# Attention and channel MLP on one core: exponentials written to SBUF, a new order of the work, kv rows added in pairs for the first batch, weights converted at other places

## The chip, the cores and the metric

The kernel runs on one core of a Trainium2 chip. The metric is the device time of one execution in microseconds; here it is the median of several runs. A core has five engines that run on their own and wait for each other through semaphores: TensorE (PE in the profile, its weight loads PEld), VectorE (DVE), ScalarE (ACT), GpSimd (POOL) and SyncE (SP, which here only issues DMAs). SBUF is the working memory, PSUM the small memory into which TensorE writes.

## The reference, cut to what matters

```python
kv_pool = kv.reshape(B, H//4, 4, W//4, 4, C).mean(axis=(2, 4))   # 16 rows averaged into one
k = v = kv_pool.reshape(B, -1, C) @ w_sr                          # 768 keys per batch
s = q @ k.T / sqrt(C)                                             # 12288 queries per batch, 4 batches
a = softmax(s)
x = a @ v
x_prev = x shifted down by one row (zeros first)
xk = mu_k*x + (1-mu_k)*x_prev;  xr = mu_r*x + (1-mu_r)*x_prev
out = sigmoid(xr @ w_r) * (relu(xk @ w_k)**2 @ w_v)               # w_k is 128x1024, w_v 1024x128
```

The inputs q, kv and w_sr are float32, the other weights float64. The output has to be more exact than one pass of TensorE's reduced float32 (`fp32r`) gives, so the kernel splits each operand into a high and a low part and adds three products.

## The kernel before, in words

The 4 x 12288 queries are cut into 96 **tiles** of 512, 24 to a batch. For one tile the work runs through these steps; the names in brackets are those of the table `WHEN`, and a digit counts the four groups of 128 queries (s) or the four pairs of 128 MLP columns (f).

- q is loaded (`qf`) and split (`qh` on ScalarE, `ql` on GpSimd).
- For each s: scores for 768 keys in PSUM, six matmuls (`S0` to `S3`); their maximum on VectorE (`nm`); the exponential with its sum on ScalarE (`ex`), written **in place into the PSUM tile S** (line 270); one over the sum (`dn`, `rc`, VectorE, one column); the probabilities as two float16 halves, the high one by ScalarE (`f1`, line 289), the low one by VectorE (`f2`, line 294), both into the tile `pp`, both reading S. So S keeps its PSUM slot until `f2` has ended. A DMA on SP's queue transposes `pp` into `pT` (`tt`, line 303).
- The product with v, three matmuls for each of six key blocks, into `px` (`AV0` to `AV5`).
- `xe` (ScalarE), `xc`, `d`, `xk`, `xr` (VectorE) mix with the row before; both are split (`xkh` VectorE, `xrh` ScalarE, `xkl` and `xrl` GpSimd).
- The MLP: for each f, `ph` in PSUM by `ha` (four matmuls with `xkh`) and `hb` (two with `xkl`); `rr` = relu on ScalarE (`r`); `kk` = `ph` x `rr` on VectorE (`k2`); `kh` = square, rounded, on ScalarE; `kl` = `kk` - `kh` on GpSimd, for f = 3 on VectorE. `kk` is the last reader of `ph`, for f = 3 `kl` is. `va` and `vb` multiply `kh` and `kl` with w_v into `pv`.
- The gate: `z` (three matmuls into `pz`), `az`, `rl`, `E`, `th` on ScalarE, `g` on VectorE; then `o` = `pv` x `g` and the store (`so`).

**PSUM.** `S`, `ph` and the batch's `pk` and `pt` share one ring of three slots (`ps_b`, line 58). Eight tiles pass through it for each tile of queries. `px` and `pz` share one slot.

**What sets the order.** `WHEN` gives each step of tile i the time `i * PERIOD + WHEN[step]`; `PERIOD` is 20.2. All steps go through a heap in the order of these planned times (lines 491 to 494), so each engine gets its instructions in that order, and steps of up to four tiles stand between each other. The times are only a sorting key: an instruction starts when its engine reaches it and its inputs and its buffer are ready. For planned times up to `FREE` = 72 the order isn't kept, and the framework's scheduler sorts these instructions by itself (`Ordered`, line 21).

**The batch's keys.** Batch 0 (`first_pool`, line 114) loads 16 tiles of 768 kv columns; TensorE multiplies and adds the first 512 columns of each tile in PSUM (`pk`), VectorE adds the other 256 (`acc`). The other batches (`later_pool`) are summed on VectorE, one `acc` reduction in each of twelve tiles of queries. `batch_prep` then splits the keys (`ks`, `ksh`, `ksl`), scales them (`am`, `ex`, `exi`, `exs`, `ivs`, `sv`, `ksv`), transposes them on TensorE (`pt`) and splits them into float16 (`v1`, `v2`).

**The weights.** w_k, w_v and w_r come as pairs of 32-bit words. `load_weights` (line 81) converts a chunk of 512 columns by six steps on VectorE (`e`, `ef`, `ei`, `m`, `ei` again, `m` again), two on ScalarE (`lf` and the high part) and three on GpSimd (`rest`, `dw`, the low part): four such chunks and one of 128 columns.

Of the kernel before, what the change touches and what calls it, by code (L numbers as in the profile page):

```python
# [39 lines left out]
def tile_kernel(ctx, tc, qT, kv0, kvw, w_sr, mu_k, mu_r, w_k, w_v, w_r, outT):  # L40
# [39 lines left out]

    def load_weights(w, hi, lo, half):

        n = w.shape[1]
        raw = prep.tile([P, n, 2], I32, name="raw", tag="kv", bufs=KV_BUFS)
        sp.dma_start(out=raw, in_=w)
        yield 4.0
# [27 lines left out]
    def first_pool(b):  # L114

        pk = ps_b.tile([P, 1024], F32, name="pk", tag="big")
        acc = prep.tile([P, K - 512], F32, name="acc", tag="acc")
        first = None
        for w in range(WIN):
# [5 lines left out]
            if w == 0:  # L125
                dve.tensor_copy(out=acc, in_=kv_t[:, 512:K])
            else:
                dve.tensor_tensor(out=acc, in0=acc, in1=kv_t[:, 512:K], op=ALU.add)
            yield 1.1
        pe.matmul(pk[:, 512:K], lhsT=wsr, rhs=acc, start=True, stop=True)  # L130
        return pk

    def later_pool(b):

# [10 lines left out]
        yield 2.0  # L145
        return pk

    def batch_prep(b, res):
# [6 lines left out]
        for c0, c1 in [(0, K)] if later else CHUNKS:  # L155
            act.activation(out=ks[:, c0:c1], in_=pk[:, c0:c1], func=AF.Copy, scale=scale / WIN)
            if later:
                yield 3.0
            dve.tensor_copy(out=ksh[:, c0:c1], in_=ks[:, c0:c1])
            if later:  # L160
                yield 3.0
            eng = pool if later else dve
            eng.tensor_tensor(
                out=ksl[:, c0:c1], in0=ks[:, c0:c1], in1=ksh[:, c0:c1].bitcast(F32), op=ALU.subtract
            )
# [306 lines left out]

    def weights(w, hi, lo, half):
        for c in range(0, w.shape[1], WC):
            cs = slice(c, min(c + WC, w.shape[1]))
            yield from load_weights(w[:, cs, :], hi[:, cs], lo[:, cs], half)
# [56 lines left out]
}  # L533
# [56 lines left out]
```

## Time and profile before

| | us |
|---|---|
| three runs | 2091.45, 2091.7, 2087.99 (median 2091.45) |
| the profiled execution | 2088.22 |
| its span, first to last instruction | 2086.4 |
| TensorE busy | 1990.4 (95%) |
| VectorE busy | 1833.1 (88%) |
| ScalarE busy | 1795.7 (86%) |
| GpSimd busy | 1071.6 (51%) |
| first scores / first `ph` of tile 0 | at 30.82 / at 80.31 |
| one tile in the steady stretch | 20.77 |
| mean granted TensorE clock | 0.989 |

A row of the timeline has the start, the duration, the engine, the source line, the operation, output<-inputs and shapes; in square brackets stands how long the engine sat idle before it and who ended that. All instructions carry L33, the helper through which they are issued, so groups are told apart by the names of their tiles. Matmuls overlap, so a start-to-start distance tells more about TensorE than a duration. A row by groups has the count, busy time in all and mean ns of one, then idle time before them. In a row by windows, busy time of PE, PEld, DVE, ACT and POOL follows the window's length, each with a count in brackets, then the granted clock, the busy share of the DMA engines and GB/s.

### The profile page before, as it was taken

What the parts mean: (1) busy time and instruction counts of PE and PEld (TensorE: products, weight loads), DVE (VectorE), ACT (ScalarE), POOL (GpSimd) and SP (SyncE); (2) the same over time, 40 slices, a digit from 0 to 9 for tenths busy, and PEclk for the clock granted to TensorE, in tenths of its full rate; (3) what the DMA queues carried; (4) which work ended last, traced back from release to release, by engine and by line L of the source; (5) the groups of instructions that cost most, each with busy time, mean ns of one, the idle gap of its engine ahead of it and who ended that gap; (6) DMA issues with size and microseconds to landing.
All of it is one profiled execution on the core that took longest, in us unless ns stands there. A gap on an engine that the chain in (4) does not pass through costs nothing.

```text
span 2086.4 us, 27449 instructions
## 1 busy us (share of the span) xinstructions
PE 1990.4 (95%) x8998; PEld 1435.8 (69%) x8998; DVE 1833.1 (88%) x2809; ACT 1795.7 (86%) x2612; POOL 1071.6 (51%) x600
## 2 busy tenths in 40 slices
PE   5799999999999999999999999999999999999998
PEld 2467676677777777667676777766767676767676
DVE  5799998888889999889898999988888898889896
ACT  2689898889898989889898888888989898989897
POOL 2455555445555555545555555554555555555555
PEclk8799999999999999999999999999999999999999
DMA  6456564555565566445555656554645454545452
GB/s 215 91 109 144 110 143 89 97 106 104 99 126 127 127 126 129 93 83 113 93 110 126 137 119 134 111 102 89 114 89 114 89 114 89 114 89 113 90 103 51
DMA packets 638544, 230.61 MB, mean 111 GB/s; under 512 B 606401, under 2 KB 606657, under 8 KB 638401
## 3 DMA queue, kind: packets, MB, share of 16 engines
q1 hardware_dynamic: 638400, 228.85, 53.9%
q8 instruction: 72, 1.18, 0.2%
q14 instruction: 72, 0.58, 0.1%
HBM read 52.63 MB, written 25.17 MB: 37 GB/s over the span
## 4 chain that ended last, share of the span: by engine, by line
PE 85%; DVE 8%; ACT 5%; DMA 1%; issue 1%; POOL 0%; POOLq 0%; DVEq 0%; SPq 0%; ACTq 0%
PE ph L33 27%; PE pv L33 26%; PE S L33 19%; PE px L33 9%; DVE kk L33 6%; ACT rr L33 5%; PE pz L33 3%; DMA kv_t<-kv 1%; PE pk L33 1%; DVE nm L33 0%; DVE m L33 0%; DVE ei L33 0%; DVE dn L33 0%; DMA raw<-moe_w_k 0%; DVE pp L33 0%
## 5 line engine op out<-in xcount | busy, mean ns | idle before, releaser
L33 POOL TENSOR_TENSOR kl<-kk,kh 128x1024 fp32r<-128x1024 f32 x288 | 689.4, 2394 | 352.5 <-DVE kk L33 196.3
L33 ACT ACTIVATE rr<-ph 128x1024 f32<-128x1024 f32 x384 | 392.7, 1023 | 107.8 <-PE ph L33 106.1
L33 PE MATMUL px<-pT,v 128*128 128x512 f16 x1728 | 441.4, 383 | 0.9 <-ACT v L33 0.9
L33 DVE TENSOR_REDUCE nm<-S 128x1 f32<-128x768 f32 x384 | 365.9, 954 | 84.1 <-PE S L33 83.5
L33 DVE TENSOR_TENSOR kk<-ph,rr 128x1024 f32<-128x1024 f32 x288 | 351.8, 1221 | 90.5 <-ACT rr L33 85.5
L33 POOL TENSOR_TENSOR xrl<-xr,xrh 128x512 fp32r<-128x512 f32 x96 | 122.7, 1278 | 598.9 <-ACT xrh L33 598.9
L33 ACT ACTIVATE S<-S,nm 128x768 f32<-128x768 f32 x384 | 331.7, 864 | 110.3 <-DVE nm L33 110.0
L33 ACT ACTIVATE kh<-rr 128x1024 fp32r<-128x1024 f32 x384 | 409.0, 1065 | 18.0 <-ACT rr L33 0.4
L33 DVE SCALAR_TENSOR_TENSOR pp<-S,rc,pp 128x768 f16<-128x768 f32 x384 | 380.3, 1011 | 12.8 <-ACT pp L33 1.5
L33 PE MATMUL ph<-xkh,wkl 128*128 128x512 f32 x768 | 331.6, 432 | 49.0 <-DVE dn L33 44.2
L33 ACT ACTIVATE pp<-S,rc 128x768 f16<-128x768 f32 x384 | 336.7, 903 | 5.1 <-ACT S L33 5.0
L33 PE MATMUL pv<-kh,wvl 128*128 128x512 f32 x768 | 304.7, 397 | 0.4 <-ACT kh L33 0.3
L33 PE MATMUL S<-ksh,ql 128*128 128x512 f32 (+1 forms) x768 | 280.5, 366 | 25.4 <-DVE pp L33 17.3
L33 PE MATMUL pv<-kh,wvh 128*128 128x512 f32 x768 | 304.5, 397 | 0.0
L33 PE MATMUL ph<-xkh,wkh 128*128 128x512 f32 x768 | 303.8, 396 | 0.0
L33 PEld LDWEIGHTS <-v 128*128 128x128 f16 x1728 | 139.0, 98 | 197.7 <-issue 80.8
L33 PE MATMUL S<-ksl,qh 128*128 128x512 f32 (+1 forms) x768 | 260.7, 339 | 0.0
L33 PE MATMUL S<-ksh,qh 128*128 128x512 f32 (+1 forms) x768 | 260.7, 339 | 0.0
L33 PE MATMUL ph<-xkl,wkh 128*128 128x512 f32 x768 | 260.2, 420 | 0.0
L33 PEld LDWEIGHTS ph<-xkh,wkl 128*128 128x128 f32 x768 | 144.6, 188 | 134.2 <-DVE dn L33 89.0
L33 PE MATMUL pv<-kl,wvh 128*128 128x512 f32 x768 | 212.2, 397 | 0.7 <-POOL kl L33 0.6
L33 PEld LDWEIGHTS S<-ksh,ql 128*128 128x128 f32 x768 | 145.6, 190 | 64.5 <-issue 26.7
(80 smaller groups left out, 2834.2 us busy)
## 6 DMA issues: line engine op xcount, KB each, us to landing
qf<-qT SPq DMA_DIRECT2D x96, 256.0 KB, 3.0
outT<-o SPq DMA_DIRECT2D x96, 256.0 KB, 3.7
kv_t<-kvw SPq DMA_DIRECT2D x36, 512.0 KB, 4.3
kv_t<-kv SPq DMA_DIRECT2D x16, 384.0 KB, 4.1
pT<-pp SPq DMA_TRANSPOSE x384, 4.2
raw<-moe_w_k SPq DMA_DIRECT2D x2, 512.0 KB, 4.7
raw<-moe_w_v SPq DMA_DIRECT2D x2, 512.0 KB, 7.2
raw<-moe_w_r SPq DMA_DIRECT2D x1, 128.0 KB, 2.0
```

The source lines that it names most:

```text
L33: ins = op(*args, **kwargs)
```

## The change

1. `ex` writes a new SBUF tile `pe` (four buffers); `f1` and `f2` read it. S is free after `ex`.
2. `WHEN` is a new table. A tile's steps are spread over a longer time (from `S0` to `vb3` 75.9 instead of 64.0 planned units), and all of them stand in another order.
3. `FREE` is -99: the table's order holds from the first instruction on.
4. For batch 0, kv is loaded two rows at a time, first 512 columns of all, then 256; VectorE adds the two (`two`), TensorE multiplies the sum: 8 + 8 float32 matmuls instead of 16 + 1. The keys' first 512 columns are split before the rest is loaded.
5. w_k is loaded between the kv loads and its conversion starts before S0; w_v and w_r are loaded together after the first q tiles, and their steps are spread, `W_GAP` = 1.8 planned units apart. `lf` comes first of a chunk's steps after `e`.
6. The kv ring has six buffers instead of four; q of the tiles after the first isn't loaded before S0; the preparation of the next batch starts two tiles later.

```diff
-    def load_weights(w, hi, lo, half):
+    def load_weights(raw, hi, lo, half, gap):
...
+    def split(c0, c1, pk, ks, ksh, ksl):
+        act.activation(out=ks[:, c0:c1], in_=pk[:, c0:c1], func=AF.Copy, scale=scale / WIN)
+        dve.tensor_copy(out=ksh[:, c0:c1], in_=ks[:, c0:c1])
+        dve.tensor_tensor(
+            out=ksl[:, c0:c1], in0=ks[:, c0:c1], in1=ksh[:, c0:c1].bitcast(F32), op=ALU.subtract
+        )
...
-            kv_t = prep.tile([P, K], F32, name="kv_t", tag="kv", bufs=KV_BUFS)
-            sp.dma_start(out=kv_t, in_=kv0[:, w, :])
-            pe.matmul(
-                pk[:, 0:512], lhsT=wsr, rhs=kv_t[:, 0:512], start=(w == 0), stop=(w == WIN - 1)
-            )
...
+        for c0, c1 in CHUNKS:
+            for w in range(0, WIN, 2):
+                kv_t = prep.tile([P, 2, c1 - c0], F32, name="kv_t", tag="kv", bufs=KV_BUFS)
+                sp.dma_start(out=kv_t, in_=kv0[:, w:w + 2, c0:c1])
+                two = work.tile([P, T], F32, name="two", tag="az", bufs=2)[:, 0:c1 - c0]
+                dve.tensor_tensor(out=two, in0=kv_t[:, 0, :], in1=kv_t[:, 1, :], op=ALU.add)
+                pe.matmul(pk[:, c0:c1], lhsT=wsr, rhs=two, start=(w == 0), stop=(w == WIN - 2))
+                yield 1.0
+            split(c0, c1, pk, ks, ksh, ksl)
...
-                    out=st[f"S{s}"][:, :K], in_=st[f"S{s}"][:, :K], func=AF.Exp,
+                    out=new(f"pe{s}", [P, K], F32), in_=st[f"S{s}"][:, :K], func=AF.Exp,
...
-                act.activation(out=pp[:, 0, :], in_=st[f"S{s}"][:, :K], func=AF.Copy, scale=st[f"rc{s}"])
+                act.activation(out=pp[:, 0, :], in_=st[f"pe{s}"], func=AF.Copy, scale=st[f"rc{s}"])
...
-                pp, pr, rc = (st[f"{x}{s}"] for x in ("pp", "S", "rc"))
+                pp, pr, rc = (st[f"{x}{s}"] for x in ("pp", "pe", "rc"))
...
-    for k, args in enumerate((
-        (w_k, wkh, wkl, False), (w_v, wvh, wvl, True), (w_r, wrh, wrl, False),
-    )):
-        steps(W_AT + T0 + 1.1 * WIN + W_STEP * k, weights(*args))
+    steps(T0 + WK_AT, weights(0.5, (w_k, wkh, wkl, False)))
+    steps(S0 + WV_AT, weights(W_GAP, (w_v, wvh, wvl, True), (w_r, wrh, wrl, False)))
...
-            steps((i + min(3, NT - 1)) * PERIOD, batch_prep(b + 1, bps[b + 1]))
+            steps((i + min(5, NT - 1)) * PERIOD, batch_prep(b + 1, bps[b + 1]))
...
-FREE = 72.0
+FREE = -99.0
...
-KV_BUFS = 4
+KV_BUFS = 6
...
-BR_AT = 14.35
+BR_AT = 15.59
...
-    "qf": -41.330, "qh": -17.482, "ql": -1.754, "S0": 4.395, "S1": 4.870, "nm0": 5.333,
+    "qf": 2.612, "qh": 19.614, "ql": 27.757, "S0": 44.210, "nm0": 50.572, "ex0": 50.578,
```

**Where the order moves instructions.** First ScalarE, before, in the steady stretch, from `r0` of one tile to its `kh1`; the rows in between are the softmax of a later tile (`S` is the score tile, now and then both in- and output, `rr` the relu, `ph` the MLP's PSUM tile):

```order
L33 ACTIVATE rr0_1205<-ph_1185 128x1024
L33 ACTIVATE kh0_1208<-rr0_1205 128x1024
L33 CAST xrh_1213<-xr_1089 128x512
L33 ACTIVATE S_1224,sm2_1252<-S_1224,nm2_1231 128x768
L33 ACTIVATE rr1_1254<-ph_1215 128x1024
L33 ACTIVATE S_1239,sm3_1258<-S_1239,nm3_1250 128x768
L33 ACTIVATE pp2_1270<-S_1224,rc2_1265 128x768
L33 ACTIVATE xe_1283<-px_1194,sv_387 128x512
L33 ACTIVATE kh1_1293<-rr1_1254 128x1024
```

And ScalarE now, the same steps:

```order
L33 ACTIVATE pe2_3265,sm2_3266<-S_3225,nm2_3237 128x768
L33 ACTIVATE pp1_3286<-pe1_3239,rc1_3261 128x768
L33 ACTIVATE rr0_3293<-ph_3232 128x1024
L33 ACTIVATE rr1_3295<-ph_3246 128x1024
L33 ACTIVATE kh0_3299<-rr0_3293 128x1024
L33 CAST qh_3306<-qf_3119 128x512
L33 ACTIVATE pe3_3310,sm3_3311<-S_3276,nm3_3304 128x768
L33 ACTIVATE pp2_3326<-pe2_3265,rc2_3274 128x768
L33 ACTIVATE pp3_3342<-pe3_3310,rc3_3330 128x768
L33 ACTIVATE xe_3345<-px_3242,sv_313 128x512
L33 ACTIVATE kh1_3349<-rr1_3295 128x1024
```

`r0` and `r1` stand one behind the other, `ex2` ahead of both, and the exponential's output is `pe`, no longer S.

VectorE before, in the steady stretch, from `f2` of one tile (`pp0`, `pp1`, second input S) to its `f2` of the third group:

```order
L33 SCALAR_TENSOR_TENSOR pp0_1409<-S_1347,rc0_1396,pp0_1409 128x768
L33 SCALAR_TENSOR_TENSOR pp1_1417<-S_1356,rc1_1411,pp1_1417 128x768
L33 TENSOR_TENSOR kk0_1439<-ph_1404,rr0_1424 128x1024
L33 TENSOR_REDUCE nm2_1450<-S_1443 128x1
L33 TENSOR_REDUCE acc_634<-kv_t_1237 128x64
L33 TENSOR_REDUCE nm3_1469<-S_1458 128x1
L33 TENSOR_SCALAR dn2_1479<-sm2_1471 128x1
L33 RECIPROCAL rc2_1484<-dn2_1479 128x1
L33 TENSOR_TENSOR kk1_1491<-ph_1434,rr1_1473 128x1024
```

And VectorE now, the corresponding stretch:

```order
L33 TENSOR_REDUCE acc_636<-kv_t_2367 128x64
L33 RECIPROCAL rc1_2594<-dn1_2585 128x1
L33 SCALAR_TENSOR_TENSOR pp0_2592<-pe0_2519,rc0_2554,pp0_2592 128x768
L33 TENSOR_SCALAR dn2_2605<-sm2_2599 128x1
L33 RECIPROCAL rc2_2607<-dn2_2605 128x1
L33 SCALAR_TENSOR_TENSOR pp1_2619<-pe1_2570,rc1_2594,pp1_2619 128x768
L33 TENSOR_TENSOR kk0_2630<-ph_2563,rr0_2626 128x1024
L33 TENSOR_REDUCE nm3_2637<-S_2609 128x1
L33 TENSOR_TENSOR kk1_2641<-ph_2577,rr1_2628 128x1024
```

`f2` takes two SBUF tiles; between `kk0` and `kk1` only `nm3` is left; the batch's reduction `acc` stands ahead of `rc1`.

VectorE now at the start, from the last adds of kv pairs to the first maximum of tile 0 (`raw_149` and `raw_151` are the chunks of w_k, `raw_230` the first of w_v); before, every weight step stood behind the last kv add:

```order
L33 TENSOR_TENSOR two_190<-kv_t_188 128x256
L33 SCALAR_TENSOR_TENSOR ei_184<-raw_149,ei_184 128x512
L33 TENSOR_TENSOR m_186<-m_186,ei_184 128x512
L33 TENSOR_TENSOR two_197<-kv_t_195 128x256
L33 TENSOR_SCALAR e_206<-raw_151 128x512
L33 TENSOR_SCALAR ef_210<-e_206 128x512
L33 CAST ksh_98<-ks_97 128x256
L33 TENSOR_TENSOR ksl_99<-ks_97,ksh_98 128x256
L33 TENSOR_SCALAR ei_228<-ef_210 128x512
L33 TENSOR_SCALAR m_238<-raw_151 128x512
L33 SCALAR_TENSOR_TENSOR ei_228<-raw_151,ei_228 128x512
L33 TENSOR_TENSOR m_238<-m_238,ei_228 128x512
```

One chunk of w_k is done, and another begun, before the keys are split; the other steps stand among tile 0's and tile 1's softmax.

More of the change, by code (lines that the diff above doesn't have):

```diff
@@ L79, in tile_kernel @@
     WC = 512
-    def load_weights(w, hi, lo, half):
[L83 to L86, printed above, removed]
+    def load_weights(raw, hi, lo, half, gap):
+        n = raw.shape[1]
         l32, h32 = raw[:, :, 0], raw[:, :, 1]
@@ L89, in load_weights @@
         dve.tensor_scalar(e, h32, 20, 0x7FF, op0=ALU.logical_shift_right, op1=ALU.bitwise_and)
+        lf = work.tile([P, n], F32, name="lf", tag="kl", bufs=3)
+        act.activation(out=lf, in_=l32.bitcast(mybir.dt.uint32), func=AF.Copy, scale=2.0 ** -52)
+        yield gap
         least = 897.0 if half else 896.0
@@ L92, in load_weights @@
         dve.tensor_scalar(ef, e, least, least + 255.0, op0=ALU.max, op1=ALU.min)
+        yield gap
         ei = work.tile([P, n], I32, name="ei", tag="kk", bufs=2)
         dve.tensor_scalar(ei, ef, least, 2.0 ** 23, op0=ALU.subtract, op1=ALU.mult)
+        yield gap
         m = work.tile([P, n], I32, name="m", tag="rr", bufs=2)
         dve.tensor_scalar(m, h32, 0xFFFFF, 3, op0=ALU.bitwise_and, op1=ALU.logical_shift_left)
-        lf = work.tile([P, n], F32, name="lf", tag="kl", bufs=3)
-        act.activation(out=lf, in_=l32.bitcast(mybir.dt.uint32), func=AF.Copy, scale=2.0 ** -52)
-        yield 2.0
+        yield gap
         dve.scalar_tensor_tensor(
@@ L102, in load_weights @@
         )
+        yield gap
         dve.tensor_tensor(out=m, in0=m, in1=ei, op=ALU.bitwise_or)
+        yield gap
         top = m.bitcast(F32)
@@ L112, in tile_kernel, with first_keys, later_keys @@
     CHUNKS = [(c, min(K, c + 512)) for c in range(0, K, 512)]
-    def first_pool(b):
-        pk = ps_b.tile([P, 1024], F32, name="pk", tag="big")
-        acc = prep.tile([P, K - 512], F32, name="acc", tag="acc")
-        first = None
-        for w in range(WIN):
-            kv_t = prep.tile([P, K], F32, name="kv_t", tag="kv", bufs=KV_BUFS)
-            sp.dma_start(out=kv_t, in_=kv0[:, w, :])
-            pe.matmul(
-                pk[:, 0:512], lhsT=wsr, rhs=kv_t[:, 0:512], start=(w == 0), stop=(w == WIN - 1)
-            )
[L125 to L133, printed above, removed]
+    def split(c0, c1, pk, ks, ksh, ksl):
[4 more added lines that the diff above has]
+        )
+    def first_keys(ks, ksh, ksl):
+        pk = ps_b.tile([P, 1024], F32, name="pk", tag="big")
+        for c0, c1 in CHUNKS:
[7 more added lines that the diff above has]
+            split(c0, c1, pk, ks, ksh, ksl)
+    def later_keys(b, ks, ksh, ksl):
         acc = prep.tile([P, K], F32, name="acc", tag="acc")
@@ L145, in later_pool @@
         yield 2.0
-        return pk
+        act.activation(out=ks, in_=pk[:, 0:K], func=AF.Copy, scale=scale / WIN)
+        yield 3.0
+        dve.tensor_copy(out=ksh, in_=ks)
+        yield 3.0
+        pool.tensor_tensor(out=ksl, in0=ks, in1=ksh.bitcast(F32), op=ALU.subtract)
     def batch_prep(b, res):
         later = b > 0
-        pk = yield from (later_pool if later else first_pool)(b)
         ks = prep.tile([P, K], F32, name="ks")
@@ L154, in batch_prep @@
         ksl = bat.tile([P, K], F32R, name="ksl")
[L155 to L165, printed above, removed]
+        yield from later_keys(b, ks, ksh, ksl) if later else first_keys(ks, ksh, ksl)
         res += [ksh, ksl]
-        yield V_WAIT
+        yield V_WAIT if later else 4.0
         am = prep.tile([P, 1], F32, name="am")
@@ L186, in batch_prep @@
         dve.tensor_scalar_mul(ksv, ks, ivs)
-        yield until(PK_AT, 4.0) if later else 1.0
+        yield until(PK_AT, 4.0) if later else 2.0
         v1 = bat.tile([P, NK, P], F16, name="v1")
@@ L221, in plan_tile, with at @@
         st = {}
-        def at(when):
+        def at(when, least=-math.inf):
             def take(fn):
-                note(i * PERIOD + when, fn)
+                note(max(i * PERIOD + when, least), fn)
             return take
@@ L231, in new @@
             return st[key]
-        @at(WHEN["qf"])
+        @at(WHEN["qf"], WHEN["S0"] if i else -math.inf)
         def _():
             sp.dma_start(out=new("qf", [P, T], F32), in_=qT[b, :, t * T:(t + 1) * T])
-        @at(WHEN["qh"])
+        @at(WHEN["qh"], WHEN["S0"] + 0.1 if i else -math.inf)
         def _():
@@ L471, in tile_kernel, with weights @@
     bps = {b: [] for b in range(B)}
[L473 to L476, printed above, removed]
+    def weights(gap, *what):
+        parts = []
+        for w, hi, lo, half in what:
+            for c in range(0, w.shape[1], WC):
+                cs = slice(c, min(c + WC, w.shape[1]))
+                raw = prep.tile([P, cs.stop - c, 2], I32, name="raw", tag="kv", bufs=KV_BUFS)
+                sp.dma_start(out=raw, in_=w[:, cs, :])
+                parts.append((raw, hi[:, cs], lo[:, cs], half, gap))
+        yield W_WAIT
+        for part in parts:
+            yield from load_weights(*part)
     S0 = WHEN["S0"]
-    T0 = S0 - 1.1 * WIN - 4.0
+    T0 = S0 - 2 * (WIN // 2) - 0.1
     steps(T0, batch_prep(0, bps[0]))
-    for k, args in enumerate((
-        (w_k, wkh, wkl, False), (w_v, wvh, wvl, True), (w_r, wrh, wrl, False),
-    )):
-        steps(W_AT + T0 + 1.1 * WIN + W_STEP * k, weights(*args))
+    steps(T0 + WK_AT, weights(0.5, (w_k, wkh, wkl, False)))
+    steps(S0 + WV_AT, weights(W_GAP, (w_v, wvh, wvl, True), (w_r, wrh, wrl, False)))
     for mu, src in ((mk, mu_k), (mr, mu_r)):
@@ L494, in tile_kernel @@
         fn()
-FREE = 72.0
-W_AT = 1.0
-W_WAIT = 5.0
-W_GAP = 1.4
+FREE = -99.0
+WK_AT = 8.1
+WV_AT = 0.1
+W_WAIT = 4.0
+W_GAP = 1.8
 V_WAIT = 16.0
```

5 lines of the change are left out of this document (2 added, 3 removed), and 30 rows, old and new, of the table WHEN.

## The prediction

> **What bounds the kernel now.** I read the page first (busy time per engine), then busy time by stretches, then the groups with what ended the idle time before them, then the timeline around the largest wait.
>
> ```profile
> PE 1990.4 (95%) x8998; PEld 1435.8 (69%) x8998; DVE 1833.1 (88%) x2809; ACT 1795.7 (86%) x2612; POOL 1071.6 (51%) x600
> ```
>
> The page's first part: TensorE is the fullest engine, but VectorE and ScalarE are not far behind. By stretches of the span:
>
> ```profile
> 0.00:30.82 30.82, 18.51 (x34) 6.23 (x35) 8.71 (x22) 3.94 (x6) 3.18 (x8) 1.00 0.83 270
> 30.82:80.31 49.49, 22.67 (x84) 16.70 (x85) 43.83 (x77) 22.90 (x40) 22.73 (x19) 0.68 0.52 111
> ```
>
> Two single periods of the steady stretch, the first with a reduction for the next batch, the second without:
>
> ```profile
> 182.27:203.04 20.77, 20.29 (x95) 14.77 (x94) 19.31 (x30) 18.54 (x27) 10.90 (x6) 1.00 0.61 127
> 980.84:1001.61 20.77, 20.29 (x95) 14.76 (x94) 18.28 (x29) 18.55 (x28) 10.90 (x7) 1.00 0.50 101
> ```
>
> After its window, a row has its length, then busy time of PE, PEld, DVE, ACT and POOL. Two things carry the time. In the steady stretch one tile (of 96) takes 20.77 us, and TensorE is busy for 20.29 of it: it is the bound, but not quite full. And until the first MLP matmul at 80.31 VectorE is the bound: 43.83 of 49.49 us.
>
> The next rows show the missing half microsecond, first as a group with its releasers, then one instance of it in the timeline.
>
> ```profile
> L33 PE MATMUL ph<-xkh,wkl 128*128 128x512 f32 x768 | 331.6, 432 | 49.0 <-DVE dn L33 44.2 <-DVE xkh L33 3.2 <-DVE kk L33 1.5
> 1016.83 0.62 PE L33 MATMUL ph<-xkl,wkh 128*128 128x512 f32 x2
> 1017.30 2.12 PE L33 MATMUL px<-pT,v 128*128 128x512 f16 x9
> 1019.90 0.50 PE L33 MATMUL ph<-xkh,wkl 128*128 128x512 f32 x1 [0.48 <-DVE dn L33]
> 1020.23 0.39 PE L33 MATMUL ph<-xkh,wkh 128*128 128x512 f32 x1
> 1020.46 0.40 PE L33 MATMUL ph<-xkh,wkl 128*128 128x512 f32 x1
> 1017.49 1.02 ACT L33 ACTIVATE rr<-ph 128x1024 f32<-128x1024 f32 x1 [0.19 <-PE ph L33]
> 1018.62 1.23 DVE L33 TENSOR_TENSOR kk<-ph,rr 128x1024 f32<-128x1024 f32 x1 [0.37 <-ACT rr L33]
> ```
>
> The wait is put down to `dn`, a tiny instruction, but what ends at 1019.85 is `kk`, the last reader of a `ph` tile (1018.62 + 1.23). So it is a wait for a PSUM slot: `hb1` fills the tile, `rr` reads it, `kk` reads it, and only then may `ha2` start: 1019.90 - 1017.30 = 2.60 us, over which the order has only nine `px` matmuls. The loss per tile is 0.48 us, and a restart of 0.10 (1019.90 to 1020.23 is 0.33, the next step 0.23).
>
> **The change part by part.** *Exponentials in SBUF, and the new order.* S now gives up its PSUM slot after `ex` instead of after `f1` and `f2`. In the new TensorE order `hb0` and `hb1` stand together, and AV2, S3, AV3, vb2, vb3 and AV4 follow before `ha2`, AV5 too before `ha3`. Lengths from neighbouring starts:
>
> ```profile
> 1011.36 0.82 PE L33 MATMUL px<-pT,v 128*128 128x512 f16 x3
> 1011.83 0.82 PE L33 MATMUL ph<-xkl,wkh 128*128 128x512 f32 x2
> 1012.49 0.82 PE L33 MATMUL px<-pT,v 128*128 128x512 f16 x3
> 1005.06 0.40 PE L33 MATMUL S<-ksh,ql 128*128 128x512 f32 x1
> 1006.11 0.39 PE L33 MATMUL S<-ksh,ql 128*128 128x512 f32 x1
> ```
>
> Three AV and two other matmuls take 1012.49 - 1011.36 = 1.13 us, 0.23 each; one S takes 1006.11 - 1005.06 = 1.05. So AV2, S3, AV3, vb2 with vb3, AV4 are 0.69 + 1.05 + 0.69 + 0.92 + 0.69 = 4.0 us. `ha2` needs `rr0` and `kk0`, the 2.60 us above: covered by 1.4. `ha3` needs `rr0`, `rr1`, then `kk0`, `nm3`, `kk1` on VectorE; from `hb1`'s end: S3 is done at 1.74, `nm3` (0.95) by about 2.9, `kk1` by 4.1, and `ha3` comes at 4.0 + `ha2` 0.92 + AV5 0.69 = 5.6. The other slots go the same way: S needs `nm` and `ex` only, 1.9 us together with no row behind it. That stall goes; what is late next is VectorE, whose rows are these:
>
> ```profile
> L33 DVE SCALAR_TENSOR_TENSOR pp<-S,rc,pp 128x768 f16<-128x768 f32 x384 | 380.3, 1011 | 12.8 <-ACT pp L33 1.5
> L33 ACT ACTIVATE S<-S,nm 128x768 f32<-128x768 f32 x384 | 331.7, 864 | 110.3 <-DVE nm L33 110.0
> L33 DVE TENSOR_REDUCE nm<-S 128x1 f32<-128x768 f32 x384 | 365.9, 954 | 84.1 <-PE S L33 83.5
> L33 DVE TENSOR_TENSOR ksl<-ks,ksh 128x512 fp32r<-128x512 f32 x1 | 0.7, 681 | 0.0
> L33 DVE TENSOR_TENSOR ksl<-ks,ksh 128x256 fp32r<-128x256 f32 x1 | 0.4, 415 | 0.0
> L33 ACT ACTIVATE kh<-rr 128x1024 fp32r<-128x1024 f32 x384 | 409.0, 1065 | 18.0 <-ACT rr L33 0.4
> L33 ACT ACTIVATE rr<-ph 128x1024 f32<-128x1024 f32 x384 | 392.7, 1023 | 107.8 <-PE ph L33 106.1
> L33 ACT ACTIVATE pz<-pz 128x512 f32<-128x512 f32 x192 | 112.1, 584 | 0.1
> L33 ACT ACTIVATE az<-pz 128x512 f32<-128x512 f32 x96 | 55.6, 580 | 0.0
> ```
>
> `f2` with both inputs in SBUF: `ksl` gives 681 + 266 = 947 ns for 768 columns, against 1011: -0.06 us, four times -0.25 per tile. `f1` from SBUF: `kh` against `rr`, +42 ns for the other source, +0.17 per tile. `ex` into SBUF: 580 ns into SBUF against 584 into PSUM, nothing. ScalarE then has 18.55 + 0.17 = 18.7 us per tile, VectorE 18.28 - 0.25 = 18.0, and 19.31 - 0.25 = 19.1 in the tiles with a reduction of the next batch (36 of 96), against TensorE's 20.2 (20.77 - 0.48 - 0.10 = 20.19; 20.29 if the restart was no loss). The Trainium skill speaks against this destination: its page "ScalarE: Activation LUTs", section "ACT is a hardware spline evaluator", says that ScalarE writes PSUM faster than SBUF. The rows 580 and 584 do not show it; by the rule `ex` would grow by an amount that the page doesn't give, and the 1.5 us that ScalarE has free per tile would take it.
>
> So the steady term is 0.48 to 0.58 us per tile. I take 0.52, since a fuller TensorE will find some small waits, over the 95 periods from the first tile's `ha0` to the last one's: -49 us, bounds -46 and -55.
>
> *The start.* `two` adds pairs on VectorE and halves TensorE's passes over kv, w_k's two transfers go between the kv loads, and its first chunk is converted before S0.
>
> ```profile
> L33 DVE TENSOR_TENSOR m<-m,ei 128x512 int32<-128x512 int32 x4 | 4.9, 1218 | 0.0
> L33 DVE TENSOR_SCALAR ei<-ef 128x512 int32<-128x512 f32 x4 | 3.3, 820 | 0.0
> L33 DVE SCALAR_TENSOR_TENSOR ei<-raw,ei 128x512 int32<-128x512 int32 x4 | 2.9, 728 | 0.0
> L33 DVE TENSOR_SCALAR m<-raw 128x512 int32<-128x512 int32 x4 | 2.9, 720 | 0.0
> L33 DVE TENSOR_SCALAR e<-raw 128x512 int32<-128x512 int32 x4 | 2.6, 654 | 1.9 <-DMA raw<-moe_w_k 1.9
> L33 DVE TENSOR_SCALAR ef<-e 128x512 f32<-128x512 int32 x4 | 2.6, 650 | 0.0
> 24.90 4.66 DMA raw<-moe_w_k
> ```
>
> ```profile
> 24.90 1.72 SPq L33 DMA_DIRECT2D raw<-moe_w_k  x2
> ```
>
> All four large chunks now lie behind the kv loads: 19.2 us of the 43.83. One whole chunk (1.22 + 0.82 + 0.73 + 0.72 + 0.65 + 0.65 = 4.8 us) and the first two steps of the next (1.3) move ahead of S0, where VectorE is busy 8.71 of 30.82 us: -6.1. The rest only changes place; it still stands ahead of tile 0's first `ha0`. The eight adds for 512 columns (0.68) and eight for 256 (0.42) come to 8.8 us, against 16 of 256 columns today (6.7): hidden under the loads. The raw transfers, 1 MB ahead of seven kv loads, cost at the 270 GB/s of the first row 3.9 us if nothing else gives; six buffers and half as many matmuls of TensorE give some back. I take S0 as unmoved, with bounds -3 and +4, and no gain from the `f2` of the first two tiles, which meet GpSimd's weight steps (below, up to +4). On SP's queue w_v's and w_r's three transfers now stand together ahead of the first `pT`: 3 x 0.86 = 2.6 us of issue (1.72 for two, above), hidden, since `f20` of tile 0 ends 0.95 + 0.86 + 0.95 = 2.8 us or more after S0 (`nm`, `ex`, itself), and the issue starts before S0. On GpSimd `ql` of tile 1 stands behind w_k's six steps; S0 of tile 1 waits longer for `ksv` and `pt` anyway. The start: -6 us, bounds -9 and +2.
>
> *The batch preparation* (two tiles later, S itself two tiles later against the plan's zero) issues the same instructions; its reduction now stands between `dn1` and `rc1`, where VectorE would otherwise wait for `rr0`. Its place in the PSUM ring can cost or save a stall like today's 2.00 us per batch:
>
> ```profile
> 395.71 0.47 PE L33 MATMUL S<-ksh,ql 128*128 128x512 f32 x1 [2.00 <-DVE v L33]
> ```
>
> Three batches: 0, bounds -6 and +6. *The end*: `vb2` and `vb3` of a tile come 12 us later after S0 in the table, but the last tile's `ha0` to the end is bound by the same chain, three `kl` on GpSimd, `o`, and the store; 0, bounds -3 and +5.
>
> Sum: -49 - 6 = -55. The profiled execution took 2088.22 us (span 2086.4), inside the three runs (2087.99 to 2091.7, median 2091.45), so 2033.
>
> **The rivals.** *Slower: VectorE waits for GpSimd.* The rows show a VectorE instruction whose operands all lie in SBUF waiting for a GpSimd instruction that has begun.
>
> ```profile
> 36.51 1.37 POOL L33 TENSOR_TENSOR rest<-lf,ei 128x512 f32<-128x512 f32 x1 [28.61 <-DVE dn L33]
> 36.68 1.75 DVE L33 TENSOR_TENSOR m<-m,ei 128x512 int32<-128x512 int32 x1
> 50.54 0.68 DVE L33 TENSOR_TENSOR m<-m,ei 128x512 int32<-128x512 int32 x1
> L33 POOL TENSOR_TENSOR kl<-kk,kh 128x1024 fp32r<-128x1024 f32 x288 | 689.4, 2394 | 352.5 <-DVE kk L33 196.3 <-ACT kh L33 149.2 <-PE pt L33 5.3
> ```
>
> The same add takes 0.68 us, or 1.75 when GpSimd began 0.17 earlier and ended at 37.88. Until now `f2` had one input in PSUM; now both are in SBUF, four per tile, 1.0 us each, beside three `kl` of 2.39 us and three smaller steps: GpSimd is busy 10.90 of 20.77. If they met by chance, an `f2` would meet a `kl` in 7.2/20.2 of cases and wait half of it (1.2), or a small step (3.7/20.2) and wait 0.6: 0.55 each, 2.2 us per tile. VectorE would have 18.0 + 2.2, and with half of its present gaps (20.77 - 18.28 = 2.5) 21.4 us per tile: 0.68 slower than now, +65 - 6, or 2147 us. It decides from about 1.5 us of waits per tile. Against it: the order. `xkl` and `xrl` wait for `xkh` and `xrh`, well ahead of `f20` and `f21`, and the first `kl` waits for `kh0` behind them, so GpSimd has nothing to run there; `f22` comes about when `kl0` ends, `f23` before `kh1` lets `kl1` go. Chance 0.10. The Trainium skill, page "SBUF — State Buffer", section "SBUF: two separate sides", states this as a rule: VectorE with two SBUF inputs and GpSimd take one port pair for a whole instruction, and the other is blocked. The rows agree for integer operands; for float32 with float16, as in `f2`, no run here shows it.
>
> *Half the gain.* The ring of three slots stalls elsewhere, say 0.26 us per tile (`hb3`, `rr3`, `kh3`, `kl3` free a slot only about 2 us before its next use): +25, 2058. Speaks for it: the old table was planned for the same period of 20.2 and came out at 20.77. Chance 0.13.
>
> *No gain in the steady stretch*, the start alone, or neither: VectorE's 19.1 us and its waits fill the period in the tiles with reductions and the ring elsewhere. 2082 to 2090. Chance 0.07, half of it within the bound.
>
> **How the numbers follow.** The forecast has 0.70: 2033, its own range from the bounds of its terms (-73 and -33), 2015 to 2055. About 0.2% (4 us) is what a measurement of this kernel can tell from no change. Faster by more: 0.70 + 0.13 + 0.04 = 0.87; same 0.03; slower 0.10. The range takes in the forecast and most of the half gain: 2015 to 2066.
>
> **What would show it.** Right: one tile takes 20.2 to 20.3 us, the wait of `ph` for VectorE is gone from the groups, first `ha0` near 74 us instead of 80.31, `f2` near 0.95 us. Wrong: `f2` with a mean well over 1.0 us (the port), a new wait of TensorE of some tenths that recurs every tile (the ring), or a first `ha0` at 80 or later.

## The result and the profile after

The changed kernel takes 2014.68 us (median of 4 runs, 2012.33 to 2015.09), the kernel before 2089.72 (the three runs of the table ahead and one more, 2087.38 to 2091.7): a ratio of 0.9639, 95% interval 0.9622 to 0.9656. The forecast was 2033 with a range of 2015 to 2066, so the time lies just below it: the sign and the mechanism came, the gain is 75 us and not 55. The profiled execution took 2014.93 us, its span 2013.2 against 2086.4.

The page's first part, engine by engine:

```profile
PE 1966.7 (98%) x8996; PEld 1430.8 (71%) x8996; DVE 1800.9 (89%) x2809; ACT 1810.1 (90%) x2612; POOL 1080.7 (54%) x600
```

Busy time by stretches: up to the first S, from there to the first MLP matmul, and one steady period.

```profile
0.00:28.81 28.81, 17.80 (x32) 7.52 (x33) 14.17 (x25) 4.24 (x6) 4.36 (x9) 0.88 0.87 297
28.81:73.83 45.02, 24.32 (x92) 17.21 (x91) 40.98 (x73) 22.20 (x40) 20.74 (x18) 0.70 0.47 100
980.64:1000.69 20.05, 20.05 (x95) 14.69 (x93) 17.89 (x29) 18.69 (x28) 10.98 (x7) 1.00 0.57 110
```

S0 starts at 28.81 (30.82 before) and the first MLP matmul at 73.83 (80.31). A period takes 20.05 us, and TensorE is busy for all of it; before it was 20.77.

The groups that the prediction priced, with the idle time ahead of each:

```profile
L33 DVE SCALAR_TENSOR_TENSOR pp<-pe,rc,pp 128x768 f16<-128x768 f32 x384 | 381.9, 1015 | 26.7 <-ACT pp L33 26.1 <-issue 0.3
L33 PE MATMUL ph<-xkh,wkl 128*128 128x512 f32 x768 | 357.0, 465 | 5.1 <-ACT pe L33 4.1 <-DVE xkh L33 0.9
L33 ACT ACTIVATE pp<-pe,rc 128x768 f16<-128x768 f32 x384 | 347.3, 933 | 11.8 <-ACT pe L33 11.2 <-DVE rc L33 0.4
L33 ACT ACTIVATE pe<-S,nm 128x768 f32<-128x768 f32 x384 | 346.8, 903 | 18.8 <-DVE nm L33 11.1
```

`ph` waits 5.1 us in all (49.0 before), so the stall of each tile is gone. `f2` takes 1015 ns (1011 before), `f1` 933 (903), `ex` 903 (864).

The last tile's `ha0` in the timeline of before; and in after's timeline the first batch's wait and, as the last row, the same `ha0`:

```profile
2068.55 0.40 PE L33 MATMUL ph<-xkh,wkl 128*128 128x512 f32 x1
```

```profile
368.78 0.82 PE L33 MATMUL pt<-ident,ksv 128*128 128x128 f32 x6
...
370.13 0.40 PE L33 MATMUL pv<-kh,wvh 128*128 128x512 f32 x1
372.96 0.50 PE L33 MATMUL S<-ksh,ql 128*128 128x512 f32 x1 [2.43 <-DVE v L33]
...
375.56 0.63 PE L33 MATMUL pv<-kh,wvl 128*128 128x512 f32 x1
375.99 0.63 PE L33 MATMUL pv<-kh,wvh 128*128 128x512 f32 x1
...
1995.34 0.47 PE L33 MATMUL ph<-xkh,wkl 128*128 128x512 f32 x1 [0.49 <-DVE xkh L33]
```

From the first `ha0` to the last one: 1988.24 us before, 1921.51 after, 66.7 less. The start gives 6.5, and from the last `ha0` to the end it is 17.85 and 17.86. That is the whole 73.2 of the span. Inside the 66.7, 95 periods x 0.714 (20.767 and 20.053, the medians over all tiles) make 67.8; the three batches cost 3.8 more than before; and the first tile's distance to the second gained 2.6 us more than a period's gain (24.10 before, 20.80 after).

The upper rows of after show a wait of the kind that the prediction left open: S waits 2.43 us for `v`, the last reader of the slot of `pt`, once for each batch, and then matmuls start every 0.43 us and not every 0.23. Over its regular periods, measured from one tile's `z` to the next one's, a batch costs 7.3 us, each of the three (6.5, 6.6 and 4.9 before).

### The profile page after: what moved, and what is told of

It reads as the page before. It is cut to its first block, busy times and chain, and to the rows that moved or that the text cites. A ratio compares the mean times of both kernels' runs of the same rounds, so it can differ in the third digit from the quotient of the medians.

```text
span 2013.2 us, 27575 instructions
## 1 busy us (share of the span) xinstructions
PE 1966.7 (98%) x8996; PEld 1430.8 (71%) x8996; DVE 1800.9 (89%) x2809; ACT 1810.1 (90%) x2612; POOL 1080.7 (54%) x600
## 4 chain that ended last, share of the span: by engine, by line
PE 93%; ACT 2%; DVE 1%; issue 0%; DVEq 0%; ACTq 0%
PE ph L33 26%; PE pv L33 26%; PE S L33 20%; PE px L33 19%; PE pz L33 3%; ACT kh L33 1%; ACT rr L33 0%; DVE kk L33 0%; ACT xe L33 0%; DVE pp L33 0%; DVE v L33 0%; DVE ph L33 0%; DVE kl L33 0%; ACT ks L33 0%; ACT v L33 0%
## 5 line engine op out<-in xcount | busy, mean ns | idle before, releaser
L33 PE MATMUL px<-pT,v 128*128 128x512 f16 x1728 | 474.4, 384 | 4.4 <-DMA pT<-pp 4.4
L33 ACT ACTIVATE rr<-ph 128x1024 f32<-128x1024 f32 x384 | 382.5, 1022 | 102.3 <-PE ph L33 101.8
L33 DVE TENSOR_TENSOR kk<-ph,rr 128x1024 f32<-128x1024 f32 x288 | 350.5, 1218 | 76.8 <-ACT rr L33 75.1
L33 DVE SCALAR_TENSOR_TENSOR pp<-pe,rc,pp 128x768 f16<-128x768 f32 x384 | 381.9, 1015 | 26.7 <-ACT pp L33 26.1
L33 ACT ACTIVATE pe<-S,nm 128x768 f32<-128x768 f32 x384 | 346.8, 903 | 18.8 <-DVE nm L33 11.1
L33 PE MATMUL ph<-xkh,wkl 128*128 128x512 f32 x768 | 357.0, 465 | 5.1 <-ACT pe L33 4.1
L33 ACT ACTIVATE pp<-pe,rc 128x768 f16<-128x768 f32 x384 | 347.3, 933 | 11.8 <-ACT pe L33 11.2
L33 PEld LDWEIGHTS <-v 128*128 128x128 f16 x1728 | 123.7, 98 | 207.3 <-issue 135.7
L33 PE MATMUL ph<-xkl,wkh 128*128 128x512 f32 x768 | 244.4, 419 | 0.0
L33 PE MATMUL pv<-kl,wvh 128*128 128x512 f32 x768 | 243.3, 419 | 0.0
L33 PEld LDWEIGHTS pv<-kl,wvh 128*128 128x128 f32 x768 | 145.2, 189 | 41.1 <-POOL kl L33 0.5
```

Source lines behind the costliest of these rows:

```text
L33: ins = op(*args, **kwargs)
```

## The experiments

**Each half of the steady change alone.** e1 is the kernel before with the exponentials in SBUF; e3 is the changed kernel with the exponentials back over S.

```diff
-                    out=st[f"S{s}"][:, :K], in_=st[f"S{s}"][:, :K], func=AF.Exp,
+                    out=new(f"pe{s}", [P, K], F32), in_=st[f"S{s}"][:, :K], func=AF.Exp,
```

(f1 and f2 read `pe`; four buffers. e3 is the reverse in the changed kernel.)

> The kernel before with one part of the change: the exponentials written to SBUF, its own order and start kept. Slot theory (the steady gain is a wait for a PSUM slot, 0.70 us per tile from start to start, and TensorE is full at 20.05 us): S gives up its slot after the exponential, so the second half's first MLP tile takes the slot of S2 (free at 1017.2 in the profile of before, by ex2) and not that of ha1 (1019.85, by kk); the period goes from 20.77 to 20.05-20.10, 95 x 0.7 = 66 us less, 2022 us (2017 to 2030), start unmoved (first MLP matmul at 80-81). Rival, the order: the slot still waits for kk1 in the old order, the period stays 20.7-20.8 and the time 2085 to 2092. Rival, the listed idle: 0.48 to 0.58 per tile is all that goes, 2034 to 2045.

Measured: 2158.81 us, slower, 1.0326 times the kernel before (1.0308 to 1.0343). The period is 21.51. The timeline of one period of e1, on TensorE, then VectorE, then GpSimd:

```profile
1005.25 2.12 PE L33 MATMUL px<-pT,v 128*128 128x512 f16 x9
1007.01 0.58 PE L33 MATMUL ph<-xkh,wkl 128*128 128x512 f32 x1
1007.43 0.39 PE L33 MATMUL ph<-xkh,wkh 128*128 128x512 f32 x1
...
1011.86 0.63 PE L33 MATMUL pv<-kl,wvh 128*128 128x512 f32 x2
1013.73 0.50 PE L33 MATMUL pz<-xrh,wrl 128*128 128x512 f32 x1 [1.24 <-DVE xk L33]
...
1006.57 1.22 DVE L33 TENSOR_TENSOR kk<-ph,rr 128x1024 f32<-128x1024 f32 x1 [0.37 <-ACT rr L33]
...
1010.86 2.15 DVE L33 SCALAR_TENSOR_TENSOR pp<-pe,rc,pp 128x768 f16<-128x768 f32 x1
1012.93 0.74 DVE L33 SCALAR_TENSOR_TENSOR xk<-px,mk,xe 128x512 f32<-128x512 f32 x1
...
1009.78 2.41 POOL L33 TENSOR_TENSOR kl<-kk,kh 128x1024 fp32r<-128x1024 f32 x1 [1.53 <-ACT kh L33]
```

All three readings of e1 miss the time. The slot stall did go: `ha2` starts at 1007.01, while `kk1` still runs (1006.57 + 1.22 = 1007.79), and from the first `px` to the second matmul of `ha2` it is 1007.43 - 1005.25 = 2.18 us, against 1020.23 - 1017.30 = 2.93 before, so the stall was 0.75 from start to start. But `f23`, now with both inputs in SBUF, takes 2.15 us, to just behind the end of GpSimd's `kl` (1009.78 + 2.41 = 1012.19); `xk` comes behind it, and `z` needs the PSUM tile that `xk` reads. This is the mechanism of the rival on the slower side, at one place of the old order, 1.1 us each time. `z` then starts 1013.73 - 1011.86 = 1.87 us after the `vb` ahead of it, against 0.47 before (1003.89 to 1004.36, rows below): 1.4 late, which carries the period from 20.05 to 21.5.

> The changed kernel with one part undone: the exponentials are written over S in PSUM again (f1 and f2 read them there), new order, new start. Slot theory: S2's slot is then held until f22, far behind S3 in VectorE's order, so S3 takes the slot of ha0 and waits for kk0; hb0, hb1, rr0, kk0 are 0.46 + 1.02 + 1.22 and waits, 2.6 to 3.3 us, over which only AV2 (0.67) stands: 2 to 2.6 us of stall per tile, and the next slots come late too; period 22 to 24, time 2200 to 2400. Rival, the order does it alone: period 20.05-20.3, time 2015 to 2040.

Measured: 2562.95 us, 1.2256 (1.2238 to 1.2274), periods of 24.7 to 27.1. Its waits of TensorE:

```profile
PE ph L33 <- DVE dn L33: 251.0, 95, 6.1
PE S L33 <- DVE kk L33: 124.5, 94, 1.7
```

The mechanism of the slot theory came (S3 waits for `kk0`, 1.3 us per tile; `ha0` waits 2.6, until `f20`, which follows the `dn` that the row names, has read S0), larger than I said: the listed waits are 3.9 us per tile, the period 4.6 to 7.1 longer than 20.05, and the granted clock of the execution 0.955 against 0.988, so matmuls also ran slower between the waits. So the new order without the SBUF exponentials is worse than the old kernel, and the exponentials in the old order are worse too. Of these two halves neither gains alone.

**How large the stall was.** e2 changes one number of the kernel before.

```diff
-"va0": 61.437
+"va0": 59.600
```

> The kernel before with one number of its table changed: va0 (four matmuls, 0.93 us of TensorE) stands ahead of ha2 and not behind it; exponentials stay in PSUM. Slot theory with a stall of 0.70 us: 0.93 us more work over the same 2.60 us covers it whole, period 20.05-20.10, time 2022 us (2017 to 2030). If the stall is only the listed idle and its restart (0.48 to 0.58): period 20.19-20.29 and 2034 to 2045. Rival, the place of the exponentials: without them in SBUF nothing changes, 2085 to 2092.

Measured: 2050.74 us, 0.9809 (0.9795 to 0.9824); the period is 20.32. The place of the stall is free (`ha2` follows `va0` at 0.23 us), and a smaller wait has come out behind it, in e2's timeline:

```profile
1008.07 0.63 PE L33 MATMUL pv<-kl,wvh 128*128 128x512 f32 x2
1008.73 0.50 PE L33 MATMUL pz<-xrh,wrl 128*128 128x512 f32 x1
1009.07 0.39 PE L33 MATMUL pz<-xrh,wrh 128*128 128x512 f32 x1
...
1007.93 0.74 DVE L33 SCALAR_TENSOR_TENSOR xk<-px,mk,xe 128x512 f32<-128x512 f32 x1
```

and the same three matmuls in before's:

```profile
1003.89 0.63 PE L33 MATMUL pv<-kl,wvh 128*128 128x512 f32 x2
1004.36 0.40 PE L33 MATMUL pz<-xrh,wrl 128*128 128x512 f32 x1
1004.59 0.39 PE L33 MATMUL pz<-xrh,wrh 128*128 128x512 f32 x1
```

1.00 us from the first to the third, against 0.70: 0.30 per tile of waiting for `xk`, which ends at 1008.67, with no idle time listed at all. That is what parts 20.32 from 20.05. So of e2's three readings the place of the exponentials is out (one number alone gained 40 us); 20.32 by itself lies near the listed idle's forecast (20.19 to 20.29), but only because the second wait took 0.30 back. So the larger part of the steady gain, 0.45 of 0.72, did not need the exponentials in SBUF; whether another order reaches 20.05 without them was not run.

**Is 20.05 TensorE's own floor?** e7 leaves out one matmul per tile.

```diff
-            pe.matmul(pz, lhsT=wrl, rhs=st["xrh"], start=True, stop=False)
-            pe.matmul(pz, lhsT=wrh, rhs=st["xrh"], start=False, stop=False)
+            pe.matmul(pz, lhsT=wrh, rhs=st["xrh"], start=True, stop=False)
```

> The changed kernel without the matmul of wrl with xrh in z, one fp32r matmul of 512 columns in each tile; the low part of w_r's product is left out of the output. If TensorE is full from start to start (20.05 = 63 x 0.2325 + 18 x 0.222 + 12 x 0.1175), the period falls by all of 0.2325 to 19.82 and the time by 96 x 0.2325 = 22 us to 1992 (1990 to 1995). Rival (VectorE or ScalarE with its waits sets 20.05 as well): the period stays, 2010 to 2015.

Measured: 1990.23 us, 0.9521 of the kernel before (0.9507 to 0.9535). One period by stretches:

```profile
996.38:1016.19 19.81, 19.81 (x94) 14.50 (x92) 17.93 (x29) 18.56 (x28) 11.00 (x7) 1.00 0.57 106
```

The period falls by 0.24, a matmul's length. TensorE is full in the changed kernel.

**The port.** e9 and e10 put a subtraction of 1024 columns on GpSimd, the one beside `f20`, the other beside `kk0`.

```diff
+                    pool.tensor_tensor(
+                        out=new("du", [P, 2 * T], F32, 1), in0=wkh[:, :2 * T].bitcast(F32),
+                        in1=wkl[:, :2 * T].bitcast(F32), op=ALU.subtract,
+                    )
```

(e9: behind `xrl`. e10: `in0=st["rr0"]`, issued with `kh1`. Both: five buffers for the kv loads.)

> The changed kernel with one more GpSimd subtraction per tile, 1024 columns (2.4 us, its result is used by nobody), behind xrl: GpSimd is idle there for 5.9 us in the profile, while VectorE runs f20 and f21 (one buffer fewer for the kv loads, to make room). Port theory: f20, whose inputs lie in SBUF, begins at 1012.9 after the subtraction (about 1012.5 to 1014.9) and lasts 2.6 to 3.0 us in place of 1.02, the mean of the four f2 goes from 1.02 to about 1.4 to 1.5 us; VectorE's idle time behind it (0.43 and 0.93) takes most of it, so the period is 20.05 to 20.4, 2013 to 2050 us. Rival (a float32 and a float16 input don't meet GpSimd): the mean stays 1.0, 20.05, 2013 to 2016.

> The same subtraction in the changed kernel, but with rr0 as an input, so that it starts when rr0 is done (996.4 in the profile) and lies beside kk0, nm3 and kk1, which read PSUM. Port theory: these three keep their 1.22, 0.95 and 1.21 us; kl0 and with it the stretch in which f22 is blocked come 0.5 us later, so f22 lasts up to 1.6 us; period 20.05 to 20.2, 2013 to 2030 us. Rival (GpSimd slows VectorE whatever it reads): kk0 lasts 2 to 3 us, its mean over the four kk goes from 1.22 to 1.5 or more, and the period rises as in e9 or more.

Measured: e9 2021.21 us, 0.9664 (0.9648 to 0.9681); e10 2016.67, 0.9644 (0.963 to 0.9659). Both keep a period of 20.05. e9's timeline, VectorE and GpSimd:

```profile
1016.93 2.75 DVE L33 SCALAR_TENSOR_TENSOR pp<-pe,rc,pp 128x768 f16<-128x768 f32 x1
...
1016.49 2.38 POOL L33 TENSOR_TENSOR du<-wkh,wkl 128x1024 f32<-128x1024 f32 x1
```

Groups of e9, then of e10:

```profile
L33 DVE SCALAR_TENSOR_TENSOR pp<-pe,rc,pp 128x768 f16<-128x768 f32 x384 | 509.3, 1347 | 2.4 <-ACT pp L33 1.6 <-issue 0.5
```

```profile
L33 DVE SCALAR_TENSOR_TENSOR pp<-pe,rc,pp 128x768 f16<-128x768 f32 x384 | 431.1, 1142 | 26.7 <-ACT pp L33 26.2 <-issue 0.3
L33 DVE TENSOR_TENSOR kk<-ph,rr 128x1024 f32<-128x1024 f32 x288 | 350.7, 1218 | 77.7 <-ACT rr L33 75.7 <-POOL kl L33 1.9
```

`f20` takes 2.75 us in place of 1.02: it is held until GpSimd is done (1016.49 + 2.38 = 1018.87) and ends 0.8 us later. `kk`, which reads PSUM, keeps 1218 ns beside the same subtraction; only `f22`, which the later `kl0` now meets, grows. The Trainium skill's page "SBUF — State Buffer", section "SBUF: two separate sides", says that a VectorE instruction with two SBUF inputs and a GpSimd one take the same ports, and that the one that starts later waits for the whole other; for a float32 with a float16 input the runs now agree (the 2.75 us). And the block cost no period: VectorE's idle 2.2 us per tile took 1.3 on the mean ((1347 - 1015) x 4; 1.7 in the tile shown). e9's 6 us more lie in the start (1.2, which is within the scatter of starts told below) and in the three batches, whose wait for `v` grew from 2.4 to 3.6 us.

**Can the old order use SBUF?** e5 and e12 are e1 with `f23` behind `xkh`, or one place further.

```diff
-"f23": 21.686
+"f23": 23.900
```

(e12: 24.450.)

> The kernel before with the exponentials in SBUF (as in e1) and one number of the old table changed: f23 stands behind xk and xkh on VectorE. Port theory for e1 (there f23 ran for 2.15 us while GpSimd ran kl from 1009.78 to 1012.19, so xk and with it z came 1.4 us late in each tile): now nothing that TensorE waits for stands behind the blocked f23 but kk2, which S1 needs about 0.3 us later than its turn; period 20.05 to 20.4 against e1's 21.5, 2022 to 2055 us. Rival (the exponentials in SBUF cost time by themselves, on ScalarE or in the slots): the period stays above 21 us, 2110 to 2160.

> The kernel before with the exponentials in SBUF and f23 one place further back than in e5: behind kk2. In e5 the wait moved to S1, which stood 0.63 us late for kk2, behind f23 (1.00) and an xkh that GpSimd's kl blocked (0.85 for 0.43). Now kk2 ends 1 us earlier, ahead of S1's turn; f23 delays kk3, nm0 and kl3, which have 0.1 to 1.5 us. Period 20.05 to 20.4 in the old order, 2022 to 2055 us. Rival (the old order can't use the free slots whatever the place of f23, because ScalarE's 0.04 us more for each exponential and f1 come late too): 20.7 or more, 2085 and up.

Measured: e5 2091.19 us, 1.0004 (0.9995 to 1.0014); e12 2087.76, 0.9987 (0.9978 to 0.9997); their periods are 20.78 and 20.77. In e5 S1 comes late, behind `kk2`; in e12 the last `vb`, behind `kl3`:

```profile
1006.50 0.28 PE L33 MATMUL S<-ksh,qh 128*128 128x256 f32 x1
1007.13 0.50 PE L33 MATMUL S<-ksh,ql 128*128 128x512 f32 x1 [0.36 <-DVE kk L33]
...
1004.16 0.85 DVE L33 CAST xkh<-xk 128x512 fp32r<-128x512 f32 x1
1004.94 1.00 DVE L33 SCALAR_TENSOR_TENSOR pp<-pe,rc,pp 128x768 f16<-128x768 f32 x1
```

```profile
1009.18 1.10 PE L33 MATMUL pv<-kl,wvh 128*128 128x512 f32 x4
1010.77 0.73 PE L33 MATMUL pv<-kl,wvh 128*128 128x512 f32 x2 [0.50 <-DVE dn L33]
...
1000.39 1.02 DVE L33 SCALAR_TENSOR_TENSOR pp<-pe,rc,pp 128x768 f16<-128x768 f32 x1 [0.15 <-ACT pp L33]
1009.51 1.21 DVE L33 TENSOR_TENSOR kl<-ph,kh 128x1024 fp32r<-128x1024 f32 x1
```

The port theory for e1 holds: out of `kl`'s way `f23` takes 1.00 us, and e1's loss against the kernel before is gone; against 20.05 half of it is left. My forecast of 20.05 to 20.4 fails twice. The rival of e12 has the number; its reason is open, since TensorE waits for VectorE there, but the head of VectorE's chain, `f22`, waits 0.15 us for ScalarE's `f1`. From there on VectorE has no gap: `f22`, `xc`, `d`, `xr`, `xk`, `xkh` (0.85 for 0.43 beside `kl`), `kk2`, `f23`, `kk3`, two `nm` and `kl3`, and the chain's end comes late wherever `f23` stands in it. That this chain sets the period is read from the rows and not tried further.

**The start.** e6 brings w_k's loads and conversion later, e11 has four buffers for the kv loads again.

```diff
-WK_AT = 8.1
+WK_AT = 13.1
```

(e11: `KV_BUFS = 4` and nothing else.)

> The changed kernel with one number of the start changed: w_k's loads and its whole conversion come 5 us later in the plan, which puts the conversion behind S0 as in the kernel before. The prediction's step (4.8 us of one chunk and 1.3 of the next were moved ahead of S0, where VectorE has room): the first MLP matmul goes from 73.8 back to 79 to 80, and the time from 2014.7 to 2020 or 2021. Rival (the start gained by the adds in pairs and the six buffers, not by w_k's place): the first MLP matmul stays within 1.5 us of 73.8, 2013 to 2016.

> The changed kernel with four buffers for the kv loads again and not six. The prediction took S0 as unmoved and it came 2.0 us earlier (30.82 to 28.81). If the buffers give that, S0 goes back to 30 to 32 and the time to 2016 to 2018; if the adds in pairs give it (TensorE's 2.1 us for each two windows before, now one pass), S0 stays within 0.5 us of 28.8 and the time at 2013 to 2016.

Measured: e6 2018.15 us, 0.9657 (0.9642 to 0.9671); e11 2017.72, 0.965 (0.9635 to 0.9664). The first MLP matmul of e6:

```profile
79.73 0.54 PE L33 MATMUL ph<-xkh,wkl 128*128 128x512 f32 x1 [4.09 <-ACT pe L33]
```

and S0 and the first MLP matmul of e11:

```profile
35.23 0.99 PE L33 MATMUL S<-ksh,ql 128*128 128x512 f32 x1
...
80.46 0.50 PE L33 MATMUL ph<-xkh,wkl 128*128 128x512 f32 x1 [4.10 <-ACT pe L33]
```

w_k's place is worth 5.9 us of start, as the prediction's 6.1 said. The buffers look worth 6.4, more than either reading of e11 had, which fits that the two raw tiles hold two of the four. But S0 scatters from execution to execution: with the new start and six buffers it came at 28.77 to 30.65 in six traces (28.81 in the changed kernel's), with the old start at 30.82 to 35.05 in five, and the kernel before's 30.82 is the earliest of these. So that the buffers bring S0 forward is clear (35.23 lies 4.6 us behind the latest of the six), the size by these traces is 4.6 to 6.5, and whether e11's S0 is later than the old start's these traces don't show. In the whole time e6 and e11 show only 3.5 and 3.0 us (2.8 and 3.4 in the profiled executions, where two of their three batches cost 5.7 us and not 7.3: the last section).

**Where the batches wait.** e4 and e8 take the slots of `pk` and `pt` at another place of the period.

```diff
-PK_AT = 64.0
+PK_AT = 14.5
```

(e8: 14.0, ahead of S2.)

> The changed kernel with one number changed: the slots that the preparation of the next batch takes (pk and pt) stand between S2 and ha0 and not ahead of S0. Slot theory: each costs its own matmuls (about 1.1 and 0.8 us) and no wait of the ring, because S0, S1 and S2 have long given up theirs there; the 7.3 us that a batch costs today falls to 2-3, three times, so 2014.7 - 13 = 2002 us (1998 to 2008), and the waits of S for v (7.3 us in all) and for ks (2.4) are gone. Rival: the waits come from the chain through ScalarE and VectorE and go with the preparation wherever it stands, 2010 to 2020.

> The changed kernel with the preparation's two slots (pk and pt) taken ahead of S2, one place earlier than in e4. Slot theory: in e4 ha1 waited 0.5 us for ex2, since the extra slot made it take S2's; here S2, ha0 and ha1 take the slots of S0, S1 and of pk itself, all free in time, so the three batches cost their own matmuls (1.1 and 0.7 us) and at most 0.3 more, against e4's 4.2: 2014.7 - 3 x (7.3 - 2.1) = 1999 (1997 to 2005). Rival (ScalarE and VectorE are too full there to read pk and pt in time): 2005 to 2012.

Measured: e4 2007.07 us, 0.9599 (0.9584 to 0.9613); e8 2001.76, 0.9577 (0.9561 to 0.9593), the fastest here, 13 us under the changed kernel. `pk` and the S behind it in e8:

```profile
334.16 1.45 PE L33 MATMUL pk<-acc,wsr 128*128 128x512 f32 x4
335.26 0.59 PE L33 MATMUL S<-ksh,ql 128*128 128x512 f32 x1
335.68 0.40 PE L33 MATMUL S<-ksl,qh 128*128 128x512 f32 x1
```

A batch costs 4.1 us in e4 and 2.8 in e8 over the regular periods, and S waits for `ks` or `v` in neither. Both lie above what was expected (2 to 3, and 2.1): in e4 two MLP matmuls of each batch wait 0.5 us for an exponential, in e8 one waits 0.3; the rest is mostly the preparation's own matmuls (1.1 us for `pk`). The rival of both, that the waits for `ks` and `v` go along wherever the preparation stands, is out.

## Why the prediction was right in sign and short in size

- **The mechanism of the steady term was right**: a PSUM slot that `kk1` gave up late; with the exponentials in SBUF it is free in time (e1), without them the new order can't run (e3).
- **Its size was the step that failed**: "The loss per tile is 0.48 us, and a restart of 0.10", taken as 0.52. It measured 0.72, or 0.75 by e1's rows at that place: 68 us and not 49, which is the miss, and the bounds of 46 and 55 were drawn from the same reading. The listed idle time counts from the listed end of the matmul before, and that end lies behind the next one's start where nothing waits (0.40 us of duration, 0.23 from start to start), so the tail counts as busy although the next could have started. The Trainium skill's page "Perfetto Trace Analysis", section "Tensor Engine Instruction (MATMUL, LD_WEIGHTS)", says that this end is an estimate; e2's 0.30 us of waiting without any listed idle agrees. The same error stood in the floor: "20.77 - 0.48 - 0.10 = 20.19". From starts, a period holds 63 fp32r matmuls of 512 columns every 0.2325 us, 12 of 256 every 0.1175, and 18 float16 ones every 0.222: 20.05, which e7 confirms (a matmul less, 0.24 us less).
- **The start** came out at 6.5 for 6, in part by luck. w_k's place was worth what was worked out (6.1; 5.9 by e6), and "I take S0 as unmoved" was 2.0 us off, inside its bounds and no more than S0's scatter; six buffers bring S0 forward (e11). The two make 7.9; where the other 1.4 went between S0 and `ha0` is not traced.
- **Batch preparation**, put at 0 with 6 either way, cost 3.8. Of it 1.5 is one more stretch at half pace (three after, two before; the last section), and 2.4 comes with the new order: 5.7 us a batch without such a stretch (e6, e11), 4.9 before. The end, put at 0, was 0.01.
- **The small prices**: `f2` "-0.06 us" did not come (1015 ns, not 947): the subtraction with two float32 inputs was no measure for a float32 and a float16 one. `f1` grew by 30 ns for 42. `ex` was put at "nothing" and grew by 39 ns, the direction that the Trainium skill's page "ScalarE: Activation LUTs", section "ACT is a hardware spline evaluator", gives; the rows of `az` and `pz`, which I set against it, don't carry over. All of it vanished in ScalarE's 1.4 free us per tile, as said.
- **The rival on the slower side** had the right mechanism (e1, e9), and the argument against it, the order, was right: in the changed kernel's steady stretch the four `f2` keep clear of `kl` (1015 ns). Its point of decision, 1.5 us of waits per tile, was no threshold: e9 carries 1.3 at no cost, while e1 loses 1.4 by 1.1, because what counts is what stands behind the blocked instruction.

## What to carry to other kernels

Measure a stall of TensorE from start to start against the same matmuls where nothing waits; a listed idle time was a lower bound here. Where a change frees a buffer and moves operands to another memory, ask of each moved operand which engine it can now meet, and re-derive the order with it: here each half alone cost 68 us or more, both together gained 75. The places where a rare step takes a slot of a tight ring deserve their own search: one number gave 13 us more (some 4.6 of it a clock that was no longer halved, as told below).
